# Later batches' keys and values loaded by pairs of heads to 128 partitions, the last tile copied by one engine, and new due dates in an attention and feed-forward kernel

## The chip, the cores and the metric

The kernel runs on one core of a Trainium2 chip. The time is device microseconds (us) of one execution; the number given for a kernel is the median of several. A profiled execution, recorded by the hardware profiler, gives the trace that is read here: its span runs from the first to the last instruction, and its own time is a little longer than the span.

## The reference

Two parts, the second on the output of the first, all in float32:

```python
batch, n_heads, seq, head_dim = (8, 8, 576, 64)      # q, k, v
k_p = k.reshape(B, H, 72, 8, D).mean(axis=3)         # keys and values averaged over 8 rows
v_p = v.reshape(B, H, 72, 8, D).mean(axis=3)
scores = scale * np.matmul(q, k_p.transpose(0, 1, 3, 2))
scores = scores - np.max(scores, axis=-1, keepdims=True)
attn = np.exp(scores)
attn = attn / (np.sum(attn, axis=-1, keepdims=True) + 1e-09)
x = np.matmul(attn, v_p)                             # to 4608 tokens x 512
h = x @ w_in                                         # 512 -> 2048
g = h * (1.0 / (1.0 + np.exp(-1.702 * h)))
return (g @ w_out)                                   # 2048 -> 512
```

## The kernel before, in words

**Number format.** The large products run on TensorE in a fast 32-bit type (fp32r in the shapes). To keep the precision, each operand is split into a high part and a rest, and a product is three matmuls: high by high, high by rest, rest by high. The rest of an activation is a subtraction ("glall", L1630: gelu output minus its high part); it may run on GpSimd or on VectorE.

**Stages.** The start (to about 40 us): keys, values and queries of batch 0 are loaded and its attention is computed, while the 8 MB of weights begin to arrive. The decode (to about 160 us): the weights are split into their parts (lines 1235 to 1290; "raw", "raws", "e", "w"), and the first two chunks of 512 tokens are multiplied by the plain way (dense, "h" at L1371, "o" at L1413). At the same time the weights are combined into sums and differences (fold, "ws", "wd"). From about 250 us each later chunk is a round of eight pairs (pair, L1551): seven products instead of eight for two by two blocks, four into a bank of PSUM called ha and three into one called hb (L1576). ha is copied out by ScalarE or VectorE (L1591), hb is added to it by VectorE (L1598), the gelu is taken twice on ScalarE (L1615 and L1623: the high part and the full value), and the rest is subtracted (L1630). The second layer's products (o, L1778 to L1780) of a pair run between the first layer's products of the next pair. A round's plan is 96 us. Attention of the next batch runs in between: keys are summed over their windows of eight (red_k, L638), masked into block form (kbd, L648), transposed on TensorE (kps, L734) and copied by ScalarE (k, L763); then the scores (sps, L856). Of each batch the last 64 tokens are kept aside; they make the ninth and last chunk. That chunk's tiles are copied from PSUM and stored in finish().

**Loads of keys and values** (fetch_main, L518). One call brings four heads' first 512 rows of k or v, eight rows of 64 numbers beside each other on one partition, to a tile kv of 128 partitions x 2 x 512. The tiles come from a ring in order. For the first two batches (TURNED = 2), each of two DMAs brings a pair of heads to all 128 partitions and one of the two columns. For the others, each of two DMAs brings the two heads of one parity to 64 of the 128 partitions, both columns. The 64 remaining rows of a batch's heads come by other loads (tl).

**The planner.** All work is handed to a class Plan as tasks: engine, estimated time, what is read and written, and a due time. Plan.order (L207) runs through the program's time by its own estimates and gives each free engine, among the tasks whose inputs are ready, the one with the earliest due time. Estimated delays between tasks are LAGS (for DMAs) and WAITS; COSTS scales the durations; SLACK sets how far due times of earlier tasks lie ahead of later ones; CHANGE is added to a TensorE task's due time when it would switch between fp32 and fp32r matmuls. SHIFTS adds a number of microseconds to the due time of the tasks of a kind ("DVE raws"), of a batch ("kv2_0", n for batches from 3 on) or of one task ("#1" is its second). All of these numbers change only the order of the instructions on each engine, and which engine takes a task that two may do. Every engine then runs its list strictly in order and waits for what an instruction needs. Only one thing more follows from the plan: in the first 58 us it fills planned gaps of TensorE with matmuls that nobody reads (warm, L1741).

The DMAs of loads are issued by SyncE (SP in the profile), those of the outputs by ScalarE, and by SyncE for the last chunk's tiles that VectorE copies.

## Time and profile before

| | us |
|---|---|
| three timed runs: lowest, median, highest | 906.96, 908.09, 910.0 |
| the profiled execution's own time | 908.36 |
| its span | 906.2 |
| TensorE (PE) busy | 888.5 |
| VectorE (DVE) busy | 633.1 |
| ScalarE (ACT) busy | 560.8 |
| GpSimd (POOL) busy | 345.7 |
| mean granted TensorE clock, of full speed | 0.999 |

In the profile's rows a line such as L1630 is a line of the kernel; names are the program's tiles with the buffer's number left out; "out<-in" says what is written and read. In a timeline row the first number is the start in us from the span's start, the second the duration, and the bracket is the idle time of the engine before the row with what ended it. SPq and ACTq are the queues on which SyncE and ScalarE issue DMAs; a row there is the time the engine takes to issue, not the transfer. In a row of grouped instructions, "x12 | 8.4, 697" means twelve of them, 8.4 us together, 697 ns on average. In a row of a window, the columns behind the bounds are the length and then the busy time of PE, the weight loads, DVE, ACT and POOL, the granted clock, the mean busy share of the 16 DMA engines, and GB/s.

### The profile page before, as it was taken

To read this page: it belongs to the slowest core of one execution; us is meant where nothing else is said; L and a number is where in the kernel's file an instruction comes from. 1 tells how busy PE (TensorE), PEld (TensorE's weight loads), DVE (VectorE), ACT (ScalarE), POOL (GpSimd) and SP (SyncE) were. 2 spreads that over 40 slices of the span, in tenths; PEclk is the share of its full clock that TensorE was granted. 3 is DMA by queue.
4 is the path that set the end of the run, shared out by engine and by line. 5 is a ranking of instruction groups with operands and counts; after the bars stand their busy time and mean duration, and the time that the engine had idled before them with its cause. 6 is when DMAs were issued, how large, how long until landed. Compare 5 with 4: busy or idle time off the path is not lost.

```text
span 906.2 us, 15947 instructions
## 1 busy us (share of the span) xinstructions
PE 888.5 (98%) x5484; PEld 792.2 (87%) x5484; DVE 633.1 (70%) x1209; ACT 560.8 (62%) x1266; POOL 345.7 (38%) x332
## 2 busy tenths in 40 slices
PE   7999999999989999999999999999999999999997
PEld 6888898888879998998999899988998989998986
DVE  6877987796887888778887787687778742222333
ACT  4987765475656675576666756685667663444433
POOL 2778667778352124223521452235222460000000
PEclk9999999999999999999999999999999999999999
DMA  9995433655467588848894888569854674567441
GB/s 263 378 383 161 123 80 95 191 195 177 145 171 211 166 225 239 235 129 233 226 251 140 227 208 243 177 202 213 234 191 137 203 253 155 183 182 225 163 140 47
DMA packets 145264, 176.69 MB, mean 195 GB/s; under 512 B 85664, under 2 KB 96928, under 8 KB 145184
## 3 DMA queue, kind: packets, MB, share of 16 engines
q1 hardware_dynamic: 140336, 166.89, 62.8%
q10 hardware_dynamic: 4848, 8.78, 2.8%
q8 instruction: 44, 0.72, 0.3%
q14 instruction: 36, 0.29, 0.1%
HBM read 150.47 MB, written 25.17 MB: 194 GB/s over the span
## 4 chain that ended last, share of the span: by engine, by line
PE 77%; DMA 2%; DVE 1%; SPq 0%; issue 0%; ACT 0%; POOL 0%; DVEq 0%; ACTq 0%; POOLq 0%
PE ha L1576 17%; PE hb L1576 13%; PE o L1780 11%; PE o L1779 11%; PE o L1778 11%; PE sps L856 3%; PE o L1415 1%; PE o L1414 1%; PE o L1413 1%; PE h L1371 1%; PE h L1373 1%; PE h L1372 1%; DMA qr<-in_q_dram 1%; PE pav L1099 1%; PE pav L1098 1%; PE pav L1096 1%
## 5 line engine op out<-in xcount | busy, mean ns | idle before, releaser
L1780 PE MATMUL o<-w,glall 128*128 128x512 f32 x448 | 176.6, 394 | 0.9 <-DVE glall L1630 0.8
L1778 PE MATMUL o<-w,ghall 128*128 128x512 f32 x448 | 176.6, 394 | 0.0
L1779 PE MATMUL o<-w,ghall 128*128 128x512 f32 x448 | 176.0, 393 | 0.0
L1630 POOL TENSOR_TENSOR glall<-shared,ghall 128x256 fp32r<-128x256 f32 x87 | 74.0, 852 | 214.6 <-ACT shared L1623 153.5
L1780 PEld LDWEIGHTS o<-w,glall 128*128 128x128 f32 x448 | 84.2, 188 | 20.4 <-DVE glall L1630 1.2
L1576 PEld LDWEIGHTS ha<-xs,ws 128*128 128x128 f32 x672 | 93.7, 189 | 8.6 <-DVE shared L1591 1.4
L1576 PE MATMUL ha<-xs,ws 128*128 128x256 f32 x672 | 98.4, 282 | 1.0 <-DVE shared L1591 1.0
L1615 ACT ACTIVATE ghall<-shared 128x256 fp32r<-128x256 f32 x150 | 61.8, 416 | 55.4 <-DVE shared L1598 32.2
L1576 PE MATMUL hb<-x,ws 128*128 128x256 f32 x672 | 95.5, 284 | 0.4 <-DVE shared L1598 0.4
L1778 PEld LDWEIGHTS o<-w,ghall 128*128 128x128 f32 x448 | 84.6, 189 | 9.1
L1779 PEld LDWEIGHTS o<-w,ghall 128*128 128x128 f32 x448 | 84.1, 188 | 9.2
L1576 PEld LDWEIGHTS hb<-x,ws 128*128 128x128 f32 x672 | 88.6, 189 | 4.0 <-DVE shared L1598 0.9
L1630 POOL TENSOR_TENSOR glall<-gall,ghall 128x256 fp32r<-128x256 f32 x48 | 39.7, 830 | 121.0 <-ACT gall L1623 83.9
L1598 DVE TENSOR_TENSOR shared<-shared,hb 128x256 f32<-128x256 f32 x112 | 46.0, 415 | 57.0 <-PE hb L1576 42.3
L1591 ACT COPY shared<-ha 128x256 f32<-128x256 f32 x91 | 33.7, 371 | 77.7 <-PE ha L1576 75.6
L1371 PE MATMUL h<-x,w 128*128 128x256 f32 (+1 forms) x192 | 63.1, 328 | 2.6 <-DVE raws L1285 1.3
L1623 ACT ACTIVATE shared<-shared 128x256 f32<-128x256 f32 x150 | 61.6, 415 | 4.6 <-ACT osb L1326 1.7
L1373 PE MATMUL h<-x,w 128*128 128x256 f32 (+1 forms) x192 | 61.2, 319 | 0.0
L1372 PE MATMUL h<-x,w 128*128 128x256 f32 (+1 forms) x192 | 61.2, 319 | 0.0
L1630 DVE TENSOR_TENSOR glall<-shared,ghall 128x256 fp32r<-128x256 f32 x63 | 34.1, 541 | 34.0 <-ACT shared L1623 26.7
L972 ACT COPY main<-sc 32x256 f32<-32x256 f32 (+2 forms) x114 | 48.8, 428 | 3.7 <-DVE sc L928 1.8
L1576 PE MATMUL ha<-x,ws 128*128 128x256 f32 x336 | 50.7, 287 | 0.0
(190 smaller groups left out, 2081.5 us busy)
## 6 DMA issues: line engine op xcount, KB each, us to landing
ws<-wd SPq DMA_DIRECT2D x168, 512.0 KB
shared<-wd SPq DMA_DIRECT2D x56, 256.0 KB
out_dram<-osb ACTq DMA_DIRECT2D x32, 256.0 KB
wd<-stage SPq DMA_DIRECT2D x16, 512.0 KB
raw<-in_moe_w_out_dram SPq DMA_DIRECT2D x15, 512.0 KB
raw<-in_moe_w_in_dram SPq DMA_DIRECT2D x15, 512.0 KB
kv_False<-in_k_dram SPq DMA_DIRECT2D x28, 256.0 KB
kv_True<-in_v_dram SPq DMA_DIRECT2D x28, 256.0 KB
```

What stands on the lines that cost most here:

```text
L972: copy(out=main()[32 * r : 32 * (r + 1), :, cols].rearrange("p j t k -> p t j k"), in_=sc()[rows, ts, a::2, 32 * half : 32 * (half + 1)],)
L1371: nc.tensor.matmul(o, lhsT=w[:, 0, j], rhs=xs[:, 0], start=j == 0, stop=False)
L1372: nc.tensor.matmul(o, lhsT=w[:, 1, j], rhs=xs[:, 0], start=False, stop=False)
L1373: nc.tensor.matmul(o, lhsT=w[:, 0, j], rhs=xs[:, 1], start=False, stop=j == NJ - 1)
L1576: nc.tensor.matmul(o, lhsT=wv()[:, r, jj], rhs=xo(k, jj), start=start and n == 0, stop=n == len(terms) - 1,  skip_group_check=not start,)
L1598: lambda: nc.vector.tensor_tensor(out=part(i), in0=part(i), in1=hb()[:, half * 256 : half * 256 + 256], op=ALU.add),
L1615: lambda: nc.scalar.activation(out=gh(), in_=src(), func=AF.Gelu_apprx_sigmoid),
L1623: lambda: nc.scalar.activation(out=part(i), in_=src(), func=AF.Gelu_apprx_sigmoid),
L1630: engine.tensor_tensor(out=gl(), in0=part(i), in1=gh().bitcast(F32), op=ALU.subtract)
L1778: nc.tensor.matmul(o(), lhsT=gh()[:, tok], rhs=w()[:, 0], start=start, stop=False)
L1779: nc.tensor.matmul(o(), lhsT=gh()[:, tok], rhs=w()[:, 1], start=False, stop=False)
L1780: nc.tensor.matmul(o(), lhsT=gl()[:, tok], rhs=w()[:, 0], start=False, stop=stop)
```

## The change

It does three things. fetch_main loads the keys and values of the batches from 2 on a pair of heads at a time to all 128 partitions; the two branches now differ only in the planner's estimate of the lag. The last tile of the last chunk, which ScalarE and VectorE copied by halves, is copied by ScalarE alone; both stores of it stay, one on SyncE's queue and one on ScalarE's. And some of the planner's constants and most of the table SHIFTS are new (245 entries before, 250 now); CHANGE goes from 3.9 to 0.

```diff
-SLACK = 0.440975
+SLACK = 0.427056
 BLOCKED = 20.0
-CHANGE = 3.9
-
-LAGS = {"kv": 4.93341, "tl": 6.58991, "qr": 4.36235, "ws": 1.76016}
-WAITS = {"early": 0.264138, "PE": 0.868087, "other": 0.213964}
+CHANGE = 0
+
+LAGS = {"kv": 4.96615, "tl": 5.8989, "qr": 4.58627, "ws": 1.42406}
+WAITS = {"early": 0.290681, "PE": 0.864626, "other": 0.213964}
-COSTS = {"DVE": 1.18114, "ACT": 1.14806, "POOL": 1.08603}
+COSTS = {"DVE": 1.181, "ACT": 1.14806, "POOL": 1.08603}
 SHIFTS = {
...
-    "DMA kv0#0": -122, "DMA kv0#1": -86.4, "DMA kv0#2": -86, "DMA kv0#3": -161.5, "DMA kv2_0": 7.5,
...
+    "ACT xtn_1": 3.9, "DMA kv0": -19.4, "DMA kv0#0": -141.4, "DMA kv0#1": -173.3, "DMA kv0#2": -177.7,
+    "DMA kv0#3": -191.2, "DMA kv0#4": 36, "DMA kv0#5": 33.5, "DMA kv0#6": 26.7, "DMA kv0#7": 22.4,
...
@@ fetch_main
-        for a in range(2):
+        for j in range(NP):
             dma(
-                KM * NP * 2048,
-                lambda a=a: nc.sync.dma_start(
-                    out=t()[a * KM : (a + 1) * KM],
-                    in_=src[b, UH * u + a : UH * (u + 1) : 2, 0 : KM * POOL].rearrange(
-                        "j (p w) d -> p j (w d)", w=POOL
+                P * 2048,
+                lambda j=j: nc.sync.dma_start(
+                    out=t()[:, j],
+                    in_=src[b, UH * u + 2 * j : UH * u + 2 * j + 2, 0 : KM * POOL].rearrange(
+                        "a (p w) d -> a p (w d)", w=POOL
                     ),
                 ),
                 writes=[ref(t)],
@@ finish
-        def copy_half(i, copy):
-            half = slice(i * DM // 2, (i + 1) * DM // 2)
-            copy(out=osb()[:, half], in_=acc()[:, half])
...
         elif last:
-            hold(dve(256, lambda: copy_half(0, nc.vector.tensor_copy), [acc], [(osb, 0)]), tile)
-            hold(act(256, lambda: copy_half(1, nc.scalar.copy), [acc], [(osb, 1)]), tile)
+            hold(act(512, lambda: nc.scalar.copy(out=osb(), in_=acc()), [acc], [osb]), tile)
```

Through the lines removed and added, a line of the kernel before is found one further down after fetch_main's loads, and four further up behind finish().

SyncE's first instructions of the program, before (in_k and in_v are the inputs; kv_137 is the tile of the keys that TensorE sums, kv_145 that of the keys that VectorE sums, tl the last 64 rows):

```order
L527 DMA kv_137<-in_k_dram 128x1x512
L527 DMA kv_145<-in_k_dram 128x1x512
L574 DMA tl_147<-in_k_dram 64x8x64
L527 DMA kv_145<-in_k_dram 128x1x512
L527 DMA kv_137<-in_k_dram 128x1x512
L1680 DMA q_0_151<-in_q_dram 128x8x64
L574 DMA tl_147<-in_v_dram 64x8x64
L1680 DMA q_0_151<-in_q_dram 128x8x64
```

And as changed:

```order
L528 DMA kv_137<-in_k_dram 128x1x512 x2
L528 DMA kv_146<-in_k_dram 128x1x512 x2
L1676 DMA q_0_149<-in_q_dram 128x8x64
L575 DMA tl_151<-in_k_dram 64x8x64
L575 DMA tl_151<-in_v_dram 64x8x64
L1676 DMA q_0_149<-in_q_dram 128x8x64
```

The two loads of kv_137 are now the first two, the first tl load has moved from the third to the sixth place, and the second tl load is the seventh DMA in both lists (the rows marked x2 count twice).

VectorE at the hand-over from the plain chunks to the pairs, near 255 to 262 us, before:

```order
L638 TENSOR_REDUCE red_k_2941<-kv_1_False 128x128
L1630 TENSOR_TENSOR glall_2964<-shared_2784,ghall_2943 128x256
L648 TENSOR_TENSOR kbd_2823<-red_k_2941,mask_84 128x256
L800 TENSOR_TENSOR vt_2921<-tbd_2754,vt_2921 32x512
L1591 COPY shared_2784<-ha_0_2768 128x256
L638 TENSOR_REDUCE red_v_3008<-kv_0_True 128x128
```

And as changed (xt and xs are the next chunk's tokens, combined by subtraction):

```order
L639 TENSOR_REDUCE red_k_2936<-kv_1_False 128x128
L1175 TENSOR_TENSOR xt_0_2612<-xt_0_2612,xt_1_2813 128x512
L1175 TENSOR_TENSOR xs_4_2957<-xt_1_2813,xs_4_2957 128x512
L801 TENSOR_TENSOR vt_2914<-tbd_2757,vt_2914 32x512
L649 TENSOR_TENSOR kbd_2835<-red_k_2936,mask_84 128x256
L1587 COPY shared_2774<-ha_0_2760 128x256
L639 TENSOR_REDUCE red_v_3006<-kv_0_True 128x128
```

The rest glall left VectorE's list here, two subtractions of 512 columns came into it, and vt stands before kbd.

GpSimd at the same place, before:

```order
L1174 TENSOR_TENSOR xt_1_2843<-xt_1_2843,xt_0_2622 128x512
L1174 TENSOR_TENSOR xs_2_2937<-xt_1_2843,xs_2_2937 128x512
L1174 TENSOR_TENSOR xt_0_2622<-xt_0_2622,xt_1_2843 128x512
L1174 TENSOR_TENSOR xs_4_2959<-xt_1_2843,xs_4_2959 128x512
L1174 TENSOR_TENSOR x_2971<-xt_0_2622,x_2971 128x512
```

And as changed:

```order
L1175 TENSOR_TENSOR xt_1_2813<-xt_1_2813,xt_0_2612 128x512
L1175 TENSOR_TENSOR xs_2_2933<-xt_1_2813,xs_2_2933 128x512
L1626 TENSOR_TENSOR glall_2959<-shared_2774,ghall_2938 128x256
L1175 TENSOR_TENSOR x_2966<-xt_0_2612,x_2966 128x512
L1626 TENSOR_TENSOR glall_3049<-shared_2774,ghall_3031 128x256
```

The rest comes behind xs_2, and the steps of xt_0 and xs_4 that stood behind xs_2 are VectorE's. Over the whole program VectorE's list gets eight instructions shorter (1209 to 1201): 14 copies of ha go to ScalarE and six rests to GpSimd. On TensorE 14 fillers before red_k become 9.

14 lines of the change are left out of this document (7 added, 7 removed), and 78 rows, old and new, of the table SHIFTS.

## The prediction

> **What bounds the kernel now.** I read the page's busy times first, then the windows of the full rounds, then TensorE's waits over the whole span, and last the timelines of the three stretches where those waits lie.
>
> ```profile
> span 906.2 us, 15947 instructions
> PE 888.5 (98%) x5484; PEld 792.2 (87%) x5484; DVE 633.1 (70%) x1209; ACT 560.8 (62%) x1266; POOL 345.7 (38%) x332
> ...
> 340.00:440.00 100.00, 100.00 (x641) 90.72 (x640) 80.81 (x157) 65.08 (x159) 33.45 (x37) 1.00 0.76 211
> ...
> 540.00:640.00 100.00, 99.73 (x642) 90.26 (x642) 77.72 (x155) 65.64 (x159) 32.14 (x35) 1.00 0.75 209
> ...
> PE h L1371 <- DVE raws L1285: 1.3, 1, 1.3
> ...
> PE ha L1576 <- DVE shared L1591: 1.0, 1, 1.0
> PE h L1371 <- DVE raw L1285: 0.8, 1, 0.8
> ...
> PE o L1780 <- DVE glall L1630: 0.8, 1, 0.8
> ...
> PE hb L1576 <- DVE shared L1598: 0.6, 2, 0.4
> ```
>
> TensorE bounds it: 17.7 us of the 906.2 us span are not busy, and in the first and the last of three windows of full rounds (second column after the length, PE) it is idle for 0.00 and 0.27 us. No matmul of the program's own work is added or removed, so the change can only move the waits. The wait view (total, times, longest) shows where they are: apart from the start (until 40 us), its largest are in the weights' decode (the two h rows) and in the hand-over to the first round of pairs (ha, o and hb). Outside these stretches there is little to win and, in the rounds, nearly only something to lose.
>
> **The change part by part.** *The last tile.* The timeline from TensorE's last matmul:
>
> ```profile
> 900.66 1.45 SPq L1334 DMA_DIRECT2D out_dram<-osb  x2
> ...
> 901.32 0.37 ACT L1338 COPY osb<-o 128x256 f32<-128x256 f32 x1 [1.48 <-PE o L1780]
> 901.72 0.42 DVE L1338 COPY osb<-o 128x256 f32<-128x256 f32 x1 [1.09 <-ACT osb L1338]
> ...
> 902.21 0.55 SPq L1342 DMA_DIRECT2D out_dram<-osb  x1
> ...
> L1332 ACT COPY osb<-o x1: 587/587/587, 899.2 to 899.2; 128x512 f32<-128x512 f32 x1
> ```
>
> The two halves did not run side by side: VectorE's began 0.03 us after ScalarE's end and names it as what it waited for. Together they reach from 901.32 to 902.14. One ScalarE copy of all 512 columns takes 0.59 us by the last row, so it ends at 901.91, 0.23 us earlier, and ScalarE's store leaves at about 901.94. SyncE's store stands behind its own two of the tile before, which hold its queue until 900.66 + 1.45 = 902.11; it leaves at about 902.13 instead of 902.21. The span ends when both have landed: a gain of 0.08 to 0.23 us. I take 0.1, since SyncE's store was already the later one.
>
> *The later batches' keys and values.* Per batch and half still two DMAs of 256 KB, now to 128 partitions each instead of two heads' 64 rows twice. The first two batches load this way before the change too. What the reductions of the 24 later loads waited for, the one late load in the chain of waits, and the bytes moved while batch 1's values came in by the 128-partition form:
>
> ```profile
>   issue: 1.0, 1
>   DMA kv_False<-in_k_dram: 0.6, 1
> ...
> 257.96 4.12 DMA kv_True<-in_v_dram
> ...
> 96.00:97.00 1.00, 1.00 (x9) 0.95 (x8) 0.28 (x1) 0.86 (x3) 0.27 (x1) 1.00 0.87 328
> ```
>
> Twenty-two of 24 reductions started without a wait, so the loads are hidden by VectorE's queue. The late pair's last DMA took 4.12 us beside a weight load and an output. At the 328 GB/s of batch 1's pair, 524 KB move in 1.6 us: the most that the form could give there is 4.1 - 1.6 = 2.5 us on one load, and of that only what TensorE waits for behind it (0.2 us, below); the least is nothing, since the packets are the same and the other traffic stays. I take 0. If the cover were gone, the 0.6 and 1.0 us in these rows are the size of what shows.
>
> A rule of the Trainium skill speaks against this form: DMA: Bandwidth & Descriptors, on why a DMA increments its semaphore by 16, says that a DMA is split over the largest number of engines, up to 16, that divides the slowest dimension of both its sides. The new source begins with the pair of heads, a dimension of 2, so it would run on two engines; the old one begins with 64. The window row disagrees: the mean busy share of all 16 engines is 0.87 there, and two engines could give no more than 0.125. By the rule the result would be the fourth rival, by the row nothing.
>
> *The start.* The rows of the first 11 us:
>
> ```profile
> 0.74 1.34 SPq L527 DMA_DIRECT2D kv<-in_k_dram  x2
> ...
> 2.80 1.28 SPq L527 DMA_DIRECT2D kv<-in_k_dram  x2
> ...
> 1.36 5.82 PE L1741 MATMUL warm<-ident 128*128 128x128 f32 x28 [1.36 <-POOL ident masks.py:199]
> 7.58 2.02 PE L616 MATMUL red_k<-kv,ident 128*128 128x128 f32 x16 [0.41 <-DMA kv<-in_k_dram]
> 9.76 1.10 PE L678 MATMUL tps<-tl,members 128*128 128x512 f32 x2 [0.16 <-DMA tl<-in_v_dram]
> ```
>
> The keys that TensorE sums (kv_137) were the first and fourth load of their kind and become the first two. Their last DMA ends its issue at 2.08 instead of 4.08, so red_k can begin about 2 us earlier, near 5.6. The fillers before it fall from 14 to 9 (18 records instead of 28); at 5.82 / 28 = 0.21 us each they end near 5.2. But the step behind it, tps, waited for the last keys' tile, and that is still the seventh DMA with the same bytes before it (the third becomes the sixth, the rest move up). tps stays at about 9.7, and all that follows it at its place. Gain 0; the bounds are 0.3 us to either side, about twice its wait of 0.16.
>
> *The due dates in the decode, 95 to 160 us.* The two h rows (1.3 and 0.8 us) end on VectorE. In the order its list there is the same but for neighbours that swap: in front of the raws step (L1285) one shift changes places with a cast, both still ahead of the same reduction. I take 0; the bounds are the whole 2.1 us and its double.
>
> *The hand-over, 250 to 268 us.*
>
> ```profile
> 258.55 0.50 PE L1780 MATMUL o<-w,glall 128*128 128x512 f32 x1 [0.81 <-DVE glall L1630]
> ...
> 262.13 0.98 PE L1576 MATMUL ha<-xs,ws 128*128 128x256 f32 x6 [1.01 <-DVE shared L1591]
> 263.31 1.25 PE L856 MATMUL sps<-k,qt 128*128 128x144 f32 x8 [0.20 <-ACT k L763]
> ...
> 257.19 1.30 DVE L1630 TENSOR_TENSOR glall<-shared,ghall 128x256 fp32r<-128x256 f32 x1
> 258.42 1.51 DVE L648 TENSOR_TENSOR kbd<-red_k,mask 128x256 f32<-128x256 f32 x1
> 259.96 1.66 DVE L800 TENSOR_TENSOR vt<-tbd,vt 32x512 fp32r<-32x512 f32 x1
> 261.65 0.42 DVE L1591 COPY shared<-ha 128x256 f32<-128x256 f32 x1
> 255.67 1.30 POOL L1174 TENSOR_TENSOR xs<-xt,xs 128x512 fp32r<-128x512 f32 x1
> 261.85 0.58 ACT L1326 COPY osb<-o 128x512 f32<-128x512 f32 x1 [2.37 <-DMA out_dram<-osb]
> 262.85 0.71 ACT L763 ACTIVATE k<-kps 128x288 f32<-128x288 f32 x2 [0.41 <-ACT osb L1326]
> ```
>
> The rest glall goes from VectorE to GpSimd, behind the xs step that ends at 256.97. With GpSimd's 0.85 us for such a rest it is done at 257.8 instead of 258.49, and TensorE's L1780 starts 0.65 us earlier. In exchange VectorE gets two subtractions of 512 columns (L1174), and vt comes before kbd. The grouped rows of the rest on GpSimd and of these four:
>
> ```profile
> L1630 POOL TENSOR_TENSOR glall<-shared,ghall 128x256 fp32r<-128x256 f32 x87 | 74.0, 852 | 214.6 <-ACT shared L1623 153.5
> ...
> L1174 DVE TENSOR_TENSOR xs<-xt,xs 128x512 fp32r<-128x512 f32 x5 | 5.7, 1154 | 0.0
> L1174 DVE TENSOR_TENSOR xt<-xt,xt 128x512 f32<-128x512 f32 x6 | 5.6, 937 | 0.2 <-POOL xt L1174 0.2
> L800 DVE TENSOR_TENSOR vt<-tbd,vt 32x512 fp32r<-32x512 f32 x7 | 5.8, 834 | 0.7 <-ACT vt L797 0.3
> L648 DVE TENSOR_TENSOR kbd<-red_k,mask 128x256 f32<-128x256 f32 x12 | 8.4, 697 | 0.0
> ```
>
> VectorE comes free for them at 257.19. 0.94 + 1.15 + 0.83 + 0.70 = 3.62 us later, at 260.8, kbd is ready (was 258.42 + 1.51 = 259.93), and with 0.42 us the copy at 261.2 (was 262.07). TensorE's key transposes follow kbd, and ha them, without a wait and 0.8 us earlier than now. Then the scores wait for k. ScalarE's k stands behind the output copy at 261.85, which waited 2.37 us for an output's DMA and is not moved, so the scores start near 263.3 as before: what the first two waits give, the third takes. With the longest durations seen in this stretch (1.30 for each subtraction, 1.66, 1.51) the copy ends at 257.19 + 5.77 + 0.42 = 263.4, 1.3 us later than now; ha slips by that, and the scores, which waited 0.2 us for k behind ha, by 1.1 us. At best the 0.2 us before the scores and the later waits on VectorE (0.6 us in two) go. Bounds: 0.2 + 0.6 = 0.8 us gained, 1.1 lost; I take 0.2 gained.
>
> *The rounds.* Fourteen ha copies go from VectorE to ScalarE and six rests to GpSimd; VectorE is 78 to 81% busy in the windows (fourth column), ScalarE 65 to 66% (fifth). That relieves the busier one, but TensorE has nothing to win there: 0, and the loss is the third rival's.
>
> The sum: 0.1 + 0 + 0 + 0 + 0.2 + 0 = 0.3 us off the profiled execution's 908.36 us, 908.06. That execution was 0.27 us above the median of the three runs, 908.09; against the median the sum gives 907.8. As each of the stretches can give more than it can take, except the rounds, I set **907.5 us**.
>
> **The rivals.** *The waits that ended on VectorE go.* The hand-over's 1.0 + 0.8 + 0.6 us, the decode's 1.3 us and the last tile's 0.2 us add up to 3.9: 904.2 us. For it: VectorE ended them all, and loses about 20 instructions. Against it: in the decode its list stands as before, and k waits for an output DMA.
>
> *ScalarE becomes late in the rounds, slower than before.* Each round ScalarE loads a table, takes the exponentials and loads the other one back:
>
> ```profile
> L908 ACT ACT_TABLE_LOAD x15 | 19.2, 1283 | 0.3
> L908 ACT ACTIVATE sc<-sc 128x1728 f32<-128x1728 f32 x7 | 11.6, 1650 | 3.7 <-DVE sc L887 3.7
> ```
>
> That is 1.28 + 1.65 + 1.28 = 4.2 us in which no ha copy is taken. A copy that was VectorE's and now stands behind them keeps a bank of TensorE's h full. It decides once that copy is later than the other bank and the outputs cover; at the 0.8 us of the waits seen at the hand-over, in six rounds, it costs 4.8 us: 912.9 us. Against it: the ha copies already on ScalarE in these rounds cost TensorE nothing.
>
> *The load runs on two engines.* At 328 GB/s for a share of 0.87, two engines give 328 / 0.87 / 8 = 47 GB/s, and a pair of 524 KB takes 11 us instead of the 4.12 seen. At the hand-over alone that is 7 us on a reduction which had no slack: 914 us or more. The window row of batch 1 speaks against it.
>
> **How the numbers follow.** Chances: about as forecast 0.57, the waits on VectorE go 0.28, ScalarE late 0.13, two engines 0.02. The range leaves out the far ends of the last three: 903.8 (a little past the first rival) to 910.4 (the forecast with 0.3, 1.1 and 1.5 us lost at the start, the hand-over and one or two rounds). A measurement of this kernel tells about 0.3% (2.7 us) from no change: faster 0.29, within 0.57, slower 0.14.
>
> **What would show it.** In the new profile: one ScalarE copy of 512 columns and SyncE's last store at most 0.1 us after its previous ones; red_k near 5.6 and tps still near 9.7; no wait of an o for a rest near 258, and the scores behind the key transposes still waiting for k; the h rows on raws still there; windows of full rounds without idle. Wrong would be a wait of ha or hb on ScalarE inside 340 to 740 us, a reduction that waits for kv, or a tps that comes earlier and draws the first dense product with it.

## The result: 18% slower, and the profile after

The changed kernel takes 1072.61 us (median of six runs, 1070.53 to 1075.26) against 907.68 us for the kernel before (six runs, 906.45 to 910.0): a ratio of 1.181, 95% interval 1.179 to 1.184. The forecast was 907.5 us. The profiled execution took 1071.71 us, its span 1069.9 us.

Busy times, bytes and the chain that ended last, from the page of the changed kernel:

```profile
span 1069.9 us, 15945 instructions
PE 935.6 (87%) x5474; PEld 827.8 (77%) x5474; DVE 619.1 (58%) x1201; ACT 559.2 (52%) x1270; POOL 339.4 (32%) x335
...
HBM read 150.47 MB, written 25.17 MB: 164 GB/s over the span
...
PE 46%; DMA 28%; DVE 4%; SPq 2%; issue 2%; ACT 1%; ACTq 0%; DVEq 0%; POOL 0%; POOLq 0%
```

The last row's counterpart in the kernel before:

```profile
PE 77%; DMA 2%; DVE 1%; SPq 0%; issue 0%; ACT 0%; POOL 0%; DVEq 0%; ACTq 0%; POOLq 0%
```

The work is the same but for ten fewer matmuls that nobody reads. TensorE's idle time rose from 17.7 to 1069.9 - 935.6 = 134.3 us, so 116.6 us of the 163.7 us are idle time, and the other 47.1 us are longer busy time (935.6 against 888.5). In the chain that ended last, DMA takes 28% of the span, against 2% before. Where the longer busy time comes from stands in the windows over the rounds, first of the kernel before, then of the changed one:

```profile
340.00:840.00 500.00, 499.73 (x3180) 452.78 (x3179) 339.78 (x690) 310.57 (x749) 149.72 (x153) 1.00 0.71 203
```

```profile
340.00:840.00 500.00, 418.42 (x2456) 373.45 (x2455) 300.12 (x610) 249.91 (x606) 123.47 (x137) 0.90 0.53 159
```

TensorE is idle for 81.6 of 500 us, and the granted clock (third column from the end) fell to 0.90: a matmul takes 418.42 / 2456 = 170 ns on average instead of 157. The stalls cost twice, once as idle time and once as a lower clock behind them: behind the stall shown below, TensorE is busy without a gap from 304 to 309 us, at a granted clock of 0.50. The waits of VectorE show who is late:

```profile
DVE red_v L639 <- DMA kv_True<-in_v_dram: 69.0, 9, 12.9
...
DVE red_k L639 <- DMA kv_False<-in_k_dram: 40.2, 8, 9.5
```

Seventeen of the 24 later reductions wait for their load, 109 us in all; before it was one, for 0.6 us. One such load, near the hand-over, in the chain of waits and on VectorE and TensorE:

```profile
286.57 0.53 SPq L542
287.10 0.05 issue
287.15 14.51 DMA kv_True<-in_v_dram
301.66 0.03 DVEq L639
...
301.74 1.87 DVE L639 TENSOR_REDUCE red_v<-kv_True 128x128 f32<-128x1024 f32 x1 [11.53 <-DMA kv_True<-in_v_dram]
303.52 0.41 DVE L1594 TENSOR_TENSOR shared<-shared,hb 128x256 f32<-128x256 f32 x1
...
303.99 0.58 PE L1572 MATMUL hb<-xs,ws 128*128 128x256 f32 x1 [9.87 <-DVE shared L1594]
```

The pair of DMAs that took 4.12 us from the start of its last issue in the kernel before takes 14.51 us. VectorE's list runs in order, so the addition of hb stands behind the reduction, and TensorE cannot write hb again: it waits 9.87 us. And this is what the chip did for most of that time, in windows of 1.5 us:

```profile
296.50:298.00 1.50, 0.00 (x0) 0.00 (x0) 0.00 (x0) 0.00 (x0) 0.00 (x0) 0.50 0.13 49
298.00:299.50 1.50, 0.00 (x0) 0.00 (x0) 0.00 (x0) 0.00 (x0) 0.00 (x0) 0.50 0.13 49
```

All five columns of the engines are zero. The only thing that moves is the load, at 49 GB/s, and the mean busy share of the 16 DMA engines is 0.13, which is 2 of 16. Each of the two moves 24.5 GB/s, a row of 2048 bytes in 84 ns.

**What the form really is.** The text on the change above says that the two branches of fetch_main now differ only in the estimate of the lag, and the prediction that the first two batches load this way already. Both are wrong. The branch of the first two batches reads the source as "a (p w) d -> p a (w d)": the 64 windows outermost, the two heads second. The changed branch reads it as "a (p w) d -> a p (w d)": the two heads outermost. One pair of letters differs, and that is the case.

### The profile page after: what moved, and what is told of

Its sections match the earlier page's. It is cut to its first block, busy times and chain, and to the rows that moved or that the text cites. A ratio compares the mean times of both kernels' runs of the same rounds, so it can differ in the third digit from the quotient of the medians.

```text
span 1069.9 us, 15945 instructions
## 1 busy us (share of the span) xinstructions
PE 935.6 (87%) x5474; PEld 827.8 (77%) x5474; DVE 619.1 (58%) x1201; ACT 559.2 (52%) x1270; POOL 339.4 (32%) x335
## 4 chain that ended last, share of the span: by engine, by line
PE 46%; DMA 28%; DVE 4%; SPq 2%; issue 2%; ACT 1%; ACTq 0%; DVEq 0%; POOL 0%; POOLq 0%
PE ha L1572 10%; DMA kv_True<-in_v_dram 10%; PE hb L1572 8%; DMA kv_False<-in_k_dram 7%; PE o L1776 6%; PE o L1775 6%; PE o L1774 6%; DMA ws<-wd 3%; DMA qr<-in_q_dram 2%; DMA tl<-in_v_dram 2%; PE sps L857 2%; DMA wd<-stage 1%; DMA tl<-in_k_dram 1%; SPq L559 1%; PE o L1411 1%
## 5 line engine op out<-in xcount | busy, mean ns | idle before, releaser
L1774 PE MATMUL o<-w,ghall 128*128 128x512 f32 x448 | 181.5, 405 | 7.1 <-ACT ghall L1611 6.4
L1775 PE MATMUL o<-w,ghall 128*128 128x512 f32 x448 | 179.8, 401 | 0.0
L1572 PE MATMUL hb<-x,ws 128*128 128x256 f32 x672 | 100.9, 295 | 11.1 <-DVE gall L1594 11.1
L1572 PE MATMUL ha<-xs,ws 128*128 128x256 f32 x672 | 103.7, 292 | 6.5 <-DVE xs L1175 3.5
L1572 PEld LDWEIGHTS ha<-xs,ws 128*128 128x128 f32 x672 | 97.4, 198 | 13.7 <-DVE xs L1175 3.7
L1572 PEld LDWEIGHTS hb<-x,ws 128*128 128x128 f32 x672 | 95.1, 202 | 16.5 <-DVE gall L1594 11.9
L1774 PEld LDWEIGHTS o<-w,ghall 128*128 128x128 f32 x448 | 87.3, 195 | 17.3 <-ACT ghall L1611 7.4
L1775 PEld LDWEIGHTS o<-w,ghall 128*128 128x128 f32 x448 | 86.8, 194 | 8.9
L1572 PE MATMUL hb<-xs,ws 128*128 128x256 f32 x336 | 54.2, 301 | 22.0 <-DVE shared L1594 19.3
L1572 PEld LDWEIGHTS hb<-xs,ws 128*128 128x128 f32 x336 | 49.6, 207 | 24.9 <-DVE shared L1594 20.4
L1619 ACT ACTIVATE shared<-shared 128x256 f32<-128x256 f32 x150 | 61.1, 415 | 14.2 <-DMA kv_True<-in_v_dram 8.9
L1367 PE MATMUL h<-x,w 128*128 128x256 f32 (+1 forms) x192 | 64.6, 336 | 3.6 <-ACT gh L1389 1.4
L639 DVE TENSOR_REDUCE red_v<-kv_True 128x128 f32<-128x1024 f32 x12 | 22.7, 1895 | 75.3 <-DMA kv_True<-in_v_dram 69.0
L1572 PE MATMUL ha<-x,ws 128*128 128x256 f32 x336 | 55.7, 307 | 9.7 <-DVE shared L1587 6.0
L1369 PE MATMUL h<-x,w 128*128 128x256 f32 (+1 forms) x192 | 62.0, 323 | 0.4 <-DVE x L1142 0.4
```

The costliest lines, as they stand in the source:

```text
L639: lambda: nc.vector.tensor_reduce(out=red(), in_=raw().rearrange("p i (w d) -> p i d w", w=POOL), axis=AX.X, op=ALU.add),
L1367: nc.tensor.matmul(o, lhsT=w[:, 0, j], rhs=xs[:, 0], start=j == 0, stop=False)
L1369: nc.tensor.matmul(o, lhsT=w[:, 0, j], rhs=xs[:, 1], start=False, stop=j == NJ - 1)
L1572: nc.tensor.matmul(o, lhsT=wv()[:, r, jj], rhs=xo(k, jj), start=start and n == 0, stop=n == len(terms) - 1,  skip_group_check=not start,)
L1619: lambda: nc.scalar.activation(out=part(i), in_=src(), func=AF.Gelu_apprx_sigmoid),
L1774: nc.tensor.matmul(o(), lhsT=gh()[:, tok], rhs=w()[:, 0], start=start, stop=False)
```

## The experiments

The runs are shown in the order in which they answer the questions: whether the load form is the cause, which property of it, and how a slow load turns into 160 us. Last come the due dates and the last tile, on which the prediction had spent its sum.

**The load form alone.** The kernel before, with only fetch_main's later branch as in the change:

```diff
-        for a in range(2):
+        for j in range(NP):
             dma(
...
-                    in_=src[b, UH * u + a : UH * (u + 1) : 2, 0 : KM * POOL].rearrange(
-                        "j (p w) d -> p j (w d)", w=POOL
...
+                    in_=src[b, UH * u + 2 * j : UH * u + 2 * j + 2, 0 : KM * POOL].rearrange(
+                        "a (p w) d -> a p (w d)", w=POOL
```

> The kernel before with nothing changed but the form of the later batches' loads of keys and values. Theory (the load does it): about as slow as the changed kernel, 1040 to 1080 us. Rival (the new due dates, or the planner's CHANGE of 0, do it, and the load only shows their lateness): 905 to 915 us. If both are needed, in between.

Measured: 1068.39 us, ratio 1.175 (1.172 to 1.177). VectorE waits 59.4 us for keys and 56.1 us for values. The load form alone does it.

**The change with the loads of before.** The same edit backwards, on the changed kernel:

> The changed kernel with the loads of before (64 partitions, two heads by parity), so the new due dates and the last tile by ScalarE alone. Theory (the load does it): 904 to 911 us, within 0.3% of the kernel before, and VectorE's reductions wait for no load. Rival (the dates do it): 1000 us or more. Here the terms of the prediction on the start, the hand-over and the last tile can be read without the load's loss: 0, -0.2 and -0.1 us were predicted.

Measured: 906.35 us, ratio 0.997 (0.995 to 0.999). Without the load form nothing of the loss is left. VectorE's later reductions still wait three times for a load, 2.1 us in all, where no wait was expected. What this run says of the prediction's own terms follows below.

**One pair of letters.** The changed kernel with the order of the dimensions that the first two batches use:

```diff
-                        "a (p w) d -> a p (w d)", w=POOL
+                        "a (p w) d -> p a (w d)", w=POOL
```

> The changed kernel with one thing different: the source of the load is read with the windows outermost and the two heads second, as batches 0 and 1 do, instead of heads outermost. Same bytes, same two DMAs, same 128 partitions, same due dates; each row of 512 numbers goes to another partition, so keys of the two heads are mixed and the result is another one: it is run for its time alone. Theory (the outermost dimension of 2 confines the load to two engines): back to 904 to 911 us, the loads land 3.3 to 6 us after issue. Rival (128 partitions, one column per DMA): 1060 us or more, 13 us per load as in the changed kernel.

Measured: 904.29 us, ratio 0.995 (0.993 to 0.997). Same bytes, same number of DMAs, same 128 partitions and same lists: the only thing changed is which dimension is outermost, and all the loss goes. The waits for loads of the later reductions fall to

```profile
  DMA kv_True<-in_v_dram: 0.2, 1
```

one wait of 0.2 us.

**The loads by themselves.** A kernel that only loads: pieces of k, one after the other, up to 128 partitions of 2048 bytes, and VectorE copies a number of each as soon as it has landed.

> Leaves the whole computation out: it only loads pieces of k one after the other, each read by a VectorE copy before the next form, three loads of each form, and stores a few numbers. Up to 128 partitions x 512 numbers (256 KB) a load; what differs is the order of the dimensions in the source. The theory (a load is split over as many DMA engines as its outermost dimension allows: 2 heads, 2 engines): with 84 ns for a packet of 2048 bytes, 128 packets over 2 engines take 64 x 84 ns = 5.4 us and over 16 engines 0.7 us, each plus one same fixed time near 2 us. So about 7.4 us for two heads outermost, 4.7 us for four, 3.3 us for eight, 2.7 us when the 64 windows or all 128 partitions are outermost; 96 packets over 3 engines 4.7 us; 100 flat partitions (10 engines) 2.8 us, 127 flat partitions (1 engine) 12.7 us. The rival (it is the number of partitions, or the strides between the two heads, or the traffic beside the load): all forms of 128 packets take the same, within 0.5 us, alone on the chip.

VectorE's timeline; the bracket is the time from the copy before, at whose end the load is issued, to the landing:

```profile
30.56 0.15 DVE L33 COPY one<-heads2x 128x1 f32<-128x1 f32 x1 [8.04 <-DMA heads2x<-in_k_dram]
...
47.11 0.15 DVE L33 COPY one<-heads2x 128x1 f32<-128x1 f32 x1 [16.33 <-DMA heads2x<-in_k_dram]
...
58.97 0.15 DVE L33 COPY one<-heads4x 128x1 f32<-128x1 f32 x1 [5.57 <-DMA heads4x<-in_k_dram]
...
68.12 0.15 DVE L33 COPY one<-heads8x 128x1 f32<-128x1 f32 x1 [4.17 <-DMA heads8x<-in_k_dram]
...
114.79 0.15 DVE L33 COPY one<-turned64x 128x1 f32<-128x1 f32 x1 [3.05 <-DMA turned64x<-in_k_dram]
...
121.02 0.15 DVE L33 COPY one<-flat 128x1 f32<-128x1 f32 x1 [2.75 <-DMA flat<-in_k_dram]
...
140.24 0.15 DVE L33 COPY one<-flat 127x1 f32<-127x1 f32 x1 [12.59 <-DMA flat<-in_k_dram]
```

And the chip while the load of 127 rows moves (the windows of the measuring kernels have only VectorE and GpSimd ahead of the clock):

```profile
129.00:138.00 9.00, 0.00 (x0) 0.00 (x0) 1.00 0.06 24
```

| outermost dimension of the source | rows | measured | expected |
|---|---|---|---|
| 2 heads | 128 | 8.04 | 7.4 |
| 3 heads | 96 | 5.83 | 4.7 |
| 4 heads | 128 | 5.57 and 5.67 | 4.7 |
| 8 heads | 128 | 4.17 and 4.37 | 3.3 |
| 64 windows (as the first batches) | 128 | 3.05 | 2.7 |
| 128 flat rows | 128 | 2.75 and 2.86 | 2.7 |
| 127 flat rows | 127 | 12.59 and 12.70 | 12.7 |

The times follow the number of rows for each engine at 84 ns, plus 2 to 3 us, if the number of engines is the outermost dimension up to 8 heads, and sixteen for 64 windows or 128 rows: 128 rows over two engines are 64 x 84 ns = 5.4 us. Five, six and seven heads of 16 rows, which the table leaves out, took 4.19 to 4.51 us, like the eight: the 16 rows for each engine are the same, the number of rows is not. A load of 100 flat rows took 2.77 and 2.84 us, 2.8 expected. The forms with two to eight heads outermost take 0.6 to 1.1 us more than expected, which these runs do not explain. With 127 flat rows, a number that no count from 2 to 16 divides, one engine does it all: the busy share of 0.06 is one of sixteen, and 24 GB/s is about what each of the two moved above. The rival, one time for all forms, falls. The Trainium skill's page DMA: Bandwidth & Descriptors, in the section on why a DMA increments its semaphore by 16, gives this rule: as many engines as the largest number up to 16 that divides the slowest dimension of both sides. The traces agree with it, 127 rows included.

The second row of the fence was not foreseen: the same two-head load took 16.33 us when the load of 127 rows was on the way beside it. The two did not use different engines.

**A load behind the slow ones.** The next kernel measures just that: a load of 128 flat rows by itself, behind two loads in the form of the first batches, and behind two in the new form.

> Leaves the whole computation out: one load of 128 flat partitions (256 KB), three times by itself, three times issued right behind two loads of the form of the first batches (64 windows outermost), three times right behind two loads of the new form (two heads outermost). Theory (a load is split over the lowest engines and every engine works its packets in order, so a load over 16 engines is only complete when its share has come through on the two busy ones): by itself 2.8 us as in the first measurement; behind two turned loads some 1.4 us of packets and their two issues later, 4 to 6 us after the first issue; behind two loads of the new form 128 + 4 more packets of 84 ns, 11 us, so 12.5 to 14 us after the first issue, though fourteen engines are free. Rival (the engines share a later load among those that are free): behind the new form as behind the turned one, 4 to 6 us.

SyncE's issues and VectorE's copies of one round of each of the last two, and a window of 5 us before the last copy:

```profile
18.91 1.19 SPq L35 DMA_DIRECT2D aheadturned<-in_k_dram  x2
...
21.82 0.15 DVE L39 COPY one<-aheadturned 128x1 f32<-128x1 f32 x1 [2.74 <-DMA aheadturned<-in_k_dram]
23.99 0.15 DVE L37 COPY one<-behindturned 128x1 f32<-128x1 f32 x1 [2.02 <-DMA behindturned<-in_k_dram]
...
38.63 1.08 SPq L35 DMA_DIRECT2D aheadtwo<-in_k_dram  x2
...
39.80 3.60 SPq L36 DMA_DIRECT2D behindtwo<-in_k_dram  x1
46.89 0.15 DVE L39 COPY one<-aheadtwo 128x1 f32<-128x1 f32 x1 [8.10 <-DMA aheadtwo<-in_k_dram]
52.87 0.15 DVE L37 COPY one<-behindtwo 128x1 f32<-128x1 f32 x1 [5.82 <-DMA behindtwo<-in_k_dram]
...
47.00:52.00 5.00, 0.04 (x1) 0.00 (x0) 1.00 0.13 50
```

The flat load lands 23.99 - 18.91 = 5.1 us after the first issue in the one case and 52.87 - 38.63 = 14.2 us in the other (13.9 to 14.2 us in the three rounds); by itself it takes 2.8 us. In the window before it lands, the busy share of the engines is 0.13, two of sixteen. So a load over all engines is complete only when its share has come through on the two busy ones, though fourteen have nothing to do. The same section of the Trainium skill says why these are always the same two: a DMA from SyncE's queue takes the lowest-numbered engines. No run here shows the engines' numbers, but both measuring kernels agree with it. Also SyncE itself is held: it needed 3.60 us to issue the flat load.

**How 13 us per load become 160 us.** Two accounts were set against each other: each reduction's wait holds up the lists behind it, or two of the sixteen engines are overfull. First only the keys' 12 tiles take the new form:

```diff
+        for j in range(NP * (src is k)):
...
+                        "a (p w) d -> a p (w d)", w=POOL
...
-        for a in range(2):
+        for a in range(2 * (src is v)):
```

> The kernel before with the new load for the keys of the later batches only (12 of 24 tiles); values load as before. Two theories of how the slow loads cost 160 us. Waits: each reduction on VectorE waits for its late load and holds up the list behind it; before, a key tile was issued 8.0 to 22.2 us before its reduction began, now it lands 13 to 14 us after issue, so ten of the twelve come late by 0.6 to 5.5 us each, some 35 us in all, and with what each delay pushes into the next load 35 to 70 us: 940 to 980 us. Capacity: the two engines are overfull; a round of 94 us has 0.76 x 94 = 71 us of packets for each engine, 5.4 us of them keys and values; those on two engines alone are 43 us, 109 us in all, over the 94; with the keys alone on two engines it is 71 - 2.7 + 21.5 = 90 us, which still fits: 907 to 918 us.

Measured: 983.62 us, ratio 1.084 (1.082 to 1.085); VectorE waits for keys eight times, 49.8 us, where ten times and some 35 us were reckoned. Half of the slow loads give 76 us, nearly half of the whole loss. Overfull engines alone predicted at most 10 us more than before, so that account falls as the only one; the waits account, 940 to 980 us, ends 4 us short of the result.

Then, with all 24 tiles in the new form as in the changed kernel, the planner is told the measured lag:

```diff
-                lag=LAGS["kv"] if b else 2.2,
+                lag=13.0,
```

> The changed kernel with one number different: the planner's estimated lag of the later batches' loads is 13 us, as measured, in place of 4.97. It plans the reductions later and other work before them; loads and engines stay the same. Waits theory (the in-order lists wait for loads that the plan thought landed): most comes back, 915 to 960 us, and VectorE's waits for keys and values fall from 109 us to under 40. Capacity theory (two of the engines carry 109 us of packets in a round of 94): little comes back, 1000 us or more.

Measured: 1012.45 us, ratio 1.115 (1.113 to 1.117). 60 us come back of 165, and the waits account, 960 us at most, falls as the only one too. The other account's range, 1000 us or more, holds the result, though over a third of the loss came back where little was to. Who waits now for a transfer:

```profile
DVE qt L841 <- DMA qr<-in_q_dram: 36.7, 7, 8.5
POOL stage L1454 <- DMA wd<-stage: 21.6, 3, 10.0
DVE stage L1454 <- DMA wd<-stage: 16.7, 3, 10.1
...
DVE red_v L639 <- DMA kv_True<-in_v_dram: 12.6, 4, 7.7
DVE tred L701 <- DMA tl<-in_k_dram: 11.4, 2, 7.8
```

The reductions wait 12.6 us instead of 109, and in their place queries (qr), staged sums (wd) and the last rows (tl) wait, none of which changed its form (that of the last rows has four heads outermost in the kernel before too). They wait as the flat load of the second measuring kernel did. The same for the keys alone, in the kernel of the run before, with a lag of 15 us for them:

> The kernel e5_keys_only with one number different: the planner's lag of the slow key loads is 15 us instead of 4.93 (they land 13 to 14 us after issue). The plan itself then ends 14 us later than that of the kernel before. Theory that with 90 us of packets in a round on the two engines the loss of e5_keys_only is the lists' waits for late keys: nearly all of its 76 us comes back but the plan's 14, 915 to 935 us. Theory that the other loads behind the slow ones are the larger part even here: 945 us or more, with VectorE waiting for queries and folded weights and not for keys.

Measured: 965.85 us, ratio 1.064 (1.063 to 1.066); 18 of the 76 us come back. Of these waits none is for keys:

```profile
DVE tred L712 <- DMA tl<-in_k_dram: 13.4, 2, 6.7
DVE qt L852 <- DMA qr<-in_q_dram: 12.0, 4, 6.0
POOL stage L1470 <- DMA wd<-stage: 10.1, 2, 8.7
```

The second account's range holds the result. So even at the 90 us of packets in a round of 94 that were estimated for the two engines, planning around the slow loads moves the wait to the loads that come behind them.

These can be late in two ways: queued behind a slow load on the two engines, or issued late. SyncE's own list runs in order too and waits for slow loads to land before it issues others. Its longest such waits in the changed kernel:

```profile
SPq L542 <- DMA kv_True<-in_v_dram: 25.2, 4, 8.7
...
SPq L1504 <- DMA kv_False<-in_k_dram: 21.7, 5, 5.3
...
SPq L596 <- DMA kv_False<-in_k_dram: 18.0, 5, 7.2
```

All its waits for these loads are 89.6 us in the changed kernel, 57.1 with the lag of 13 us, and 15.0 in the kernel before, where the longest row was

```profile
SPq L595 <- DMA kv_True<-in_v_dram: 5.0, 7, 1.3
```

The loss is that of slow loads on two engines: first seen by the reductions, and by whoever comes next if these are put off. How it divides between the two, how much of the second is SyncE's late issue, and how much of the remaining time is the longer plan (14 us longer for the keys alone by the planner's own estimate), these runs do not separate.

**A form that keeps the pairs.** Each pair by two DMAs, one per head:

```diff
...
-                    out=t()[:, j],
-                    in_=src[b, UH * u + 2 * j : UH * u + 2 * j + 2, 0 : KM * POOL].rearrange(
-                        "a (p w) d -> a p (w d)", w=POOL
+            for a in range(2):
...
+                        out=t()[a * KM : (a + 1) * KM, j],
+                        in_=src[b, UH * u + 2 * j + a, 0 : KM * POOL].rearrange("(p w) d -> p (w d)", w=POOL),
```

> The changed kernel with each pair of heads loaded by two DMAs, one per head (64 windows outermost, to 64 partitions of one column), so the tile is filled pair by pair as in the change, with the right keys in the right places, but no DMA has two heads outermost. Four DMAs of 128 KB for a tile in place of two of 256 KB. Theory (the outermost dimension of 2): as the changed kernel with the loads of before, 904 to 911 us; the extra issues (48 at some 0.55 us on SyncE, 26 us over the whole span) lie in SyncE's waiting time. Rival (pair by pair to both halves is what is slow): 1060 us or more. If SyncE's issues matter: 908 to 915 us.

Measured: 915.67 us, ratio 1.009 (1.007 to 1.010): the loss of 165 us is gone, which again names the outermost dimension, but it is slower than 911, and just above the 915 that SyncE's issues were given. Its profiled execution, the slowest of the six, lost some 2.8 us of its span of 915.9 us at the start: the first dense product began at 41.68 us, against 38.88 in the run with the loads of before, and the granted clock was 0.5 behind TensorE's gap there (the clock is the third column from the end):

```profile
10.00:12.00 2.00, 0.89 (x1) 0.50 (x2) 0.18 (x1) 0.00 (x0) 0.00 (x0) 0.59 1.05 315
12.00:14.00 2.00, 2.00 (x7) 1.28 (x6) 0.69 (x1) 0.37 (x1) 0.00 (x0) 0.50 1.17 307
...
18.00:22.00 4.00, 3.48 (x15) 3.07 (x14) 1.93 (x4) 2.92 (x6) 1.69 (x2) 0.50 1.09 347
```

The run with the loads of before, whose gap at the start is as long, kept the clock in the same windows:

```profile
12.00:14.00 2.00, 1.87 (x16) 1.61 (x16) 0.71 (x2) 1.34 (x4) 0.00 (x0) 1.00 1.12 329
```

The rest cannot be put down to SyncE's issues alone: the planner saw four DMAs where there were two, and ordered the lists of all engines anew. What that cost and what the issues cost is not separated.

And this kernel with the last keys' load at the start moved ahead:

```diff
-    "DMA raw#4": -21.3, "DMA raw#6": -2.5, "DMA tl0": -164.2, "DMA tl0#0": 26.9, "DMA tl0#1": 16.6,
+    "DMA raw#4": -21.3, "DMA raw#6": -2.5, "DMA tl0": -179, "DMA tl0#0": 26.9, "DMA tl0#1": 16.6,
```

> The kernel e3_per_head with one due date different (tl0 from -164.2 to -179), which moves the load of the last keys at the start ahead of one query load, to the fifth place. All engines' lists but SyncE's stay as they are. If the 1.4 us by which tps comes later than in the kernel before is due to the two tl loads standing side by side, tps moves back from 11.2 to about 10 us; by the first dense product half a us of the 0.5 lost is regained, which the times can't tell: 904 to 911 us, the same as e3_per_head within 0.2%.

Measured: 917.94 us, ratio 1.011 (1.009 to 1.012), outside the range, and 0.25% above the run before, where it was to be within 0.2%. The move did nothing for tps, which began at 11.18 us instead of 11.11. That the two tl loads stand side by side is not why tps is late.

**The start's gap filled.** The changed kernel with the loads of before, and 14 unread matmuls ahead of tps:

```diff
                 done = t.begun + t.us
+            if t.name == "PE tps0#0":
+                for _ in range(14):
+                    keep_warm()
             t.emit()
```

> The kernel e2_old_load with 14 unread matmuls before tps, where TensorE stands idle for 3.4 us at the start. In the profile of e2_old_load the granted clock stayed at 1.00 there, in those of e3_per_head and e4_order it fell to 0.5 behind that gap, for 13.7 and 3.4 us. Theory (the gap puts the clock at risk, which then costs up to 3 us): the clock stays at 1.00 over the first 40 us, tps keeps its time, 11.15 us, and the time is that of e2_old_load or a little better, 903 to 907 us, with less spread than its 904.5 to 909.1. Rival (the clock is lost elsewhere or the fillers push tps): 906 to 910 us.

Measured: 908.09 us, ratio 1.000 (0.999 to 1.001), spread 905.57 to 911.8. In the profiled execution, the slowest of the twelve, tps began at 11.21 us; the clock was 1.00 to 22 us, but 0.79 in the window from 22 to 30 us, and 0.95 from 240 to 275 us. The rival's range holds the result: the fillers win nothing, and in that execution the clock was lost elsewhere.

**Due dates alone, and the keys in the good form.** Two runs for what is left of the change. The dates and constants with the old loads and the last tile by halves:

> The change's due dates and constants alone: the loads of before and the last tile by halves, as before. e2_old_load gave 0.997 (0.995 to 0.999) with these dates and the last tile by ScalarE; e9_fillers, the same lists with fillers at the start, gave 1.000. If the dates give what e2_old_load showed: 904 to 907 us, a ratio of 0.996 to 0.999. If that was luck with the granted clock: 907 to 909 us, a ratio of 0.999 to 1.002. The last tile may change 0.2 us at most.

Measured: 906.3 us, ratio 0.998 (0.997 to 0.999). And the change's loads for the keys with the windows outermost, which needs the first batches' mask and order of transposes for a right result:

```diff
+        if src is k:
+            for j in range(NP):
...
+                            "a (p w) d -> p a (w d)", w=POOL
...
-                in1=(mask2i if b < TURNED else mask2).unsqueeze(1).unsqueeze(3).broadcast_to([P, NP, 2, D]),
+                in1=(mask2i if b < TURNED or nm[0] == "k" else mask2).unsqueeze(1).unsqueeze(3).broadcast_to([P, NP, 2, D]),
...
-                        keys.rearrange("p a s -> p s a") if b < TURNED else keys,
+                        keys.rearrange("p a s -> p s a"),
```

> The kernel e2_old_load with the keys of the later batches loaded a pair of heads at a time to all 128 partitions, but with the windows outermost in the source, as the first batches do it, and the mask and the order of the key transposes of the first batches, so the result is the reference's; values as in the kernel before. The order of every engine's list is that of e2_old_load. Theory (only the outermost dimension mattered; the 128-partition form itself gives or costs nothing that can be told): 903 to 908 us, keys landing 3.4 to 6 us after issue, as in e2_old_load within 0.3%. Rival (the transposes into strided places, or the row order, cost something in each round): 909 to 915 us.

Measured: 905.7 us, ratio 0.998 (0.997 to 0.999). Both beat the kernel before by 0.2%, and the changed kernel by some 15.5%. Loading the keys by pairs to 128 partitions is worth nothing that can be told beyond the dates. For the dates there are three results, 0.997, 0.998 and, with the fillers, 1.000, and with the mixed rows of the run with one pair of letters changed 0.995; their intervals reach from 0.993 to 1.001. The gain is 0.2% or so, and no size of it is shown more closely.

## Why the prediction was wrong, point by point

**The step that failed.** Of the later batches' loads the prediction said that "the first two batches load this way before the change too", took the window of batch 1 (0.87 of 16 engines, 328 GB/s) as a measurement of the new form, and set the term to 0 with at most 2.5 us to gain. The row was right, and it was of another form: windows outermost. With it the argument against the Trainium skill's rule fell too. The rule gave the right answer, and the one row that spoke against it did not bear on it. The run with one pair of letters changed shows this by itself: 904.29 us against 1072.61.

**The fourth rival** named the mechanism, two engines, with a chance of 0.02. Its size was wrong as well. It gave 11 us for a pair, where the chain of waits has twelve of 12.9 to 17.7 us, but it counted one load, at the hand-over, for 7 us and "914 us or more". The term that was mis-sized is the number of loads: all 24 tiles take the form, 17 of their reductions wait, and the loads behind them wait as well. At the hand-over it had the mechanism right: the load, the reduction, the list behind it.

**A wait of zero is not a measure of slack.** The prediction read "twenty-two of 24 reductions started without a wait" as "hidden", without the time by which each load was early. The keys alone showed the price: 49.8 us of waits.

The other terms can be read from the run with the loads of before, whose profiled execution took 905.92 us, 2.4 us less than the 908.36 us profiled before.

**The start** (0 predicted, 0.3 us to either side). red_k was to begin near 5.6 and tps to stay at 9.7; red_k began at 5.36, but

```profile
11.15 1.10 PE L679 MATMUL tps<-tl,members 128*128 128x512 f32 x2 [3.42 <-DMA tl<-in_v_dram]
```

tps came 1.4 us later, by one profile against one. Three more profiles have the start of the kernel before (the load alone, the keys alone, and the keys alone with a lag of 15 us), and there tps began at 10.32 to 10.49 us, so about half of the 1.4 us is scatter. In the eight profiles with the new start and no fillers before tps it began at 10.62 to 11.26 us; between the medians, 10.36 and 11.13 us, lies 0.8 us. The seventh place and the same bytes did not give the same time, and why was not found (the run with the tl load moved ahead excludes the neighbour). By the first dense product nothing can be told: 38.88 against 38.40 us, where the four profiles with the old start have 38.06 to 39.42. So the 0 stands, but the bounds, made from one wait of one profile, were narrower than the scatter, and the gap of 3.4 us is a risk for the clock that the prediction did not see.

**The decode** (0 predicted): right. The two h waits stand at 1.3 and 0.8 us as before.

**The hand-over** (0.2 us gained predicted, at most 0.8): the mechanism was right, the size was not.

```profile
260.05 0.44 PE L735 MATMUL kps<-ident,kbd 128*128 128x128 f32 x2 [0.38 <-DVE kbd L649]
260.38 0.97 PE L1572 MATMUL ha<-xs,ws 128*128 128x256 f32 x6
262.26 1.25 PE L857 MATMUL sps<-k,qt 128*128 128x144 f32 x8 [0.90 <-ACT k L764]
...
258.87 0.34 ACTq L1328 DMA_DIRECT2D out_dram<-osb  x1
260.77 0.59 ACT L1327 COPY osb<-o 128x512 f32<-128x512 f32 x1 [1.93 <-DMA out_dram<-osb]
```

The wait of o for a rest and that of ha are gone, and the scores wait for k behind the output copy, as said. VectorE's list came to its two subtractions at 255.62 us, not 257.19, so kbd was ready at 260.0 us instead of the 260.8 of the sum. But the output copy starts at 260.77 instead of 261.85: the output DMA for which it waits was issued at 258.87 instead of 259.50 and waited for 1.93 us instead of 2.37. "What the first two waits give, the third takes" was the step that failed here; it took the output's DMA as fixed, and it moved with the work before it. The scores start at 262.26 instead of 263.31, 1.05 us earlier, 0.9 of it won since the first ha (241.00 against 241.17), and the two waits of hb, 0.6 us, are gone too, which the prediction had as the far end of its bounds.

**The last tile** (0.1 us predicted): nothing. One ScalarE copy of 0.59 us came as expected, and ScalarE's store left 1.05 us after the last matmul's start instead of 1.29. SyncE's left at 1.27 instead of 1.33, and from the last matmul's end to the end of the span it is 5.04 us against 4.97.

**The rounds** (0 predicted): with the old loads TensorE is idle for 0.6 us from 340 to 440 and for 0.04 us from 440 to 740. Of this 0.47 us is one wait of the scores for ScalarE's k, at 356.85; no ha or hb waits for ScalarE there. The rival of the late ScalarE, 4.8 us, has nothing more for it.

The first rival, "the waits on VectorE go, 904.2 us", is in part what remains of the change once the load is put right: 906.35 and 906.3 us lie between it and the forecast, nearer to the forecast.

## What to carry to other kernels

Read the access pattern of a transfer from its outermost dimension before its bytes: a dimension of 2 there put the whole load on two engines here, and a load over all engines that was issued behind it waited for these two. When a row of the profile is used as evidence that a form is harmless, compare the two forms letter by letter first; here "p a" and "a p" were read as one. And a load that nobody waits for is hidden only up to the time by which it is early, so that time belongs beside the wait.

## What the runs showed of the hardware that was not expected

A load over all DMA engines takes 14.2 us instead of 2.8 when two loads of two heads were issued just before it, so that one transfer's form sets the time of others. A load of 127 flat rows takes 12.6 us, one of 128 rows 2.8. And TensorE's granted clock can fall to 0.5 at an idle stretch of about 3 us: of the eight profiles in which TensorE waits 2.5 to 4.3 us for tps, five lost it between 10 and 12 us, two of them for 13.7 us, which took some 2.8 us, and three for 3.4 us; the other three kept 1.00, and so did, up to 22 us, the five in which that wait is under 0.5 us or filled. Which of the two happens at such a gap was not found to depend on anything that was changed.
